# Key and query stacks of a transformer block: twelve SBUF-to-SBUF pieces, or three writes to DRAM and four reads back

## The chip, the cores and the metric

The kernel runs on one core of a Trainium2 chip. A core has TensorE (matrix multiplication; PE in the profile, its weight loads PEld), VectorE (DVE), ScalarE (ACT), GpSimd (POOL) and SyncE (SP), which here only issues transfers, and 16 DMA engines that carry them. The metric is the device time of one execution in microseconds. All times are of that chip; the profile is one execution recorded by the hardware.

## The reference

A pre-norm block with 2048 tokens, width 1024, 32 heads of 32, hidden width 3584, in float32. Its first part is attention over four segments of 512 tokens, with a memory matrix M carried from segment to segment:

```python
q, k, v = (x @ wq), (x @ wk), (x @ wv)        # per head, per segment of 512 tokens
for s in range(4):
    p = softmax(qs @ ks.T * Dh**-0.5 + causal_mask)
    a_dot = p @ vs
    a_mem = (phi(qs) @ M) / (phi(qs) @ z + 1e-6)
    o = g * a_mem + (1 - g) * a_dot
    M, z = M + phi(ks).T @ vs, z + phi(ks).sum(0)
h = x + concat(o) @ wo                         # x is layernormed before the projections
out = h + gelu(layernorm(h) @ w1 + b1) @ w2 + b2
```

The change concerns only `qs @ ks.T`, and only how its two operands get into place.

## The kernel before

**Precision.** Products that need more than the multiplier's reduced float32 format (fp32r) are made from halves: a value is split into `hi` (rounded to fp32r) and `lo` (the rest), and a product is hi·hi + hi·lo + lo·hi. In the projections these are three matmuls (`mm3`, L114–117). For the logits of one head the contraction has only 32 rows, so the three products are laid into one contraction of 96 rows: the key stack of a head holds its 32 rows of kh, kl, kh one under the other, the query stack those of qh, qh, ql. One matmul of 96 rows, L541, then gives all three products summed.

**Tiles.** The projections come out as `kps`, `qps`, `vps`: 128 rows (four heads of 32) by 512 tokens. ACT writes kh (L413) and qh (L427) out of PSUM, DVE makes kl (L414) and ql (L428). A head's rows lie at partitions 32j to 32j+31 there, and must be brought to partitions 0–31, 32–63 and 64–95 of that head's stack. Compute engines do not do that here; `stack` (L372) does it by transfers: for each of four heads a tile of 96 x 512 (`ks` or `qs`, five buffers each), filled by three DMAs of 32 x 512 (64 KB, L377), so twelve DMAs a stack, all issued by SP.

**Loops.** The attention runs in two halves of 1024 tokens, `attention(half)`. Within a half it goes over eight groups of four heads, and for each group over two segments `sl` = 0, 1. A pair of group and segment is a unit: 16 units in a half, 32 in all, with one key stack and one query stack each, 64 stacks. Units with `sl` 0 are called even here, those with `sl` 1 odd.

**What runs beside what.** `dense(g, sl, ws, u)` makes the projections of a unit in 24 steps, k, q and v in eight chunks of three matmuls. `heads(prev)` computes the attention of the unit before, head after head, in six small steps each (PLAN, L31). The two are interleaved one to one: while TensorE projects unit u it also does the logits, transposes and products of unit u − 1. `dense` calls for the key stack at the first chunk of the query projection and for the query stack at the first chunk of the value projection. Both are read first when the next unit begins, by the `qk` of head 0. In each half the first unit has no previous heads; it runs beside the layer norm of the other segment, and its stacks are needed soon after.

**Order.** A framework planned the instruction order of each engine when the kernel was built; on the chip each engine goes through its own list in that order and waits on semaphores. The SP list carries, beside the stacks: the weight blocks `wr<-wk/wq/wv` (L326, 512 KB each, two buffers, one trio per group, so in the odd units, each waiting until POOL or DVE has split the block whose buffer it takes, L92), the store of a unit's result `o_dram<-ot` (L609, 256 KB), rows of x for the residual (`ht`, L696), and at the end of a half the reads `orr<-o_dram` (L683) and the output weights `wr<-wo` (L700). Later parts of the kernel, the output projection and the two-layer perceptron, use the same queue but no stacks; they fill the time after about 500 us to 890 us and after 1400 us.

Of the kernel before, what the change touches and what calls it, by code (L numbers as in the profile page):

```python
# [10 lines left out]
F32 = mybir.dt.float32  # L11
# [28 lines left out]
def raw(ap):  # L40
    return ap.bitcast(F32)


def build(tc, x, wq, wk, wv, wo, beta, w1, b1, w2, b2, out):
    nc = tc.nc
    top = ExitStack()
    const = top.enter_context(tc.tile_pool(name="const", bufs=1))
    dram = top.enter_context(tc.tile_pool(name="dram", bufs=1, space=DRAM))
# [33 lines left out]
    p1_dram = [dram.tile([P, 512], F32, name=f"p1_dram{j}") for j in range(FB // 2)]  # L82
    h_dram = [[dram.tile([S // P, P, FB // 4, P], F32, name=f"h_dram{i}{s}") for s in range(2)] for i in range(2)]

    acts = {}

    def split(pool, w, hi, lo, hi_eng="vector", lo_eng="gpsimd"):
# [99 lines left out]
    def hooked(gen, fn, every, count):  # L187
        for n, _ in enumerate(gen):
            if n % every == every - 1 and n // every < count:
                fn(n // every)  # L190
            yield
# [152 lines left out]
    def attention(half, first):  # L344
# [26 lines left out]

        def stack(a, b, name, order):  # L372
            out = []
            for j in range(4):
                st = ab.tile([96, 512], F32R, tag=name, name=name, bufs=5)
                for blk, src in enumerate(order):
                    nc.sync.dma_start(raw(st[32 * blk:32 * blk + 32, :]), raw((a, b)[src][32 * j:32 * j + 32, :]))  # L377
                out.append(st)
            return out

# [21 lines left out]
        def dense(g, sl, ws, u):  # L402
# [15 lines left out]
            for c in project(ws["q"], sl, "qps", qps):  # L418
                if c == 0:
                    u["ks"] = stack(kh, kl, "ks", (0, 1, 0))  # L420
                if c == 2 and s < 3:
                    zc = ab.tile([P, 64], F32, name="zc", bufs=2)[:, 0:1]
                    pk = phi_sum(kparts, "pk", zc)
                next(behind, None)
                yield
# [7 lines left out]
            for c in project(ws["v"], sl, "vps", vps):  # L433
                if c == 0:
                    u["qs"] = stack(qh, ql, "qs", (0, 0, 1))
                if s > 0:
                    if c == 2:
                        pq = phi_sum(qparts, "pq")
                    if c == 4:
                        while small:  # L440
                            one_small()
                        pqh, pql = tmpr("pqh"), tmpr("pql")
                        mzh = ab.tile([P, 256], F32R, name="mzh", bufs=1)[:, 0:132]
                        mzl = ab.tile([P, 256], F32R, name="mzl", bufs=1)[:, 0:132]
                        nc.scalar.copy(pqh, pq)
                        nc.gpsimd.tensor_copy(mzh, MZ[:, g, :])
                        nc.gpsimd.tensor_tensor(mzl, MZ[:, g, :], raw(mzh), op=ALU.subtract)
                    if c == 5:
                        nc.gpsimd.tensor_tensor(pql, pq, raw(pqh), op=ALU.subtract)
                if c == 1 and s < 3:  # L450
                    pkn = ps_dense("pkn")
                    for i in range(4):
                        nc.tensor.transpose(pkn[:, i * P:(i + 1) * P], pk[:, i * P:(i + 1) * P], ident)
                    pkh, pkl = tmpr("pkh"), tmpr("pkl")
                    nc.scalar.copy(pkh, pkn)
                if c == 2 and s < 3:
                    nc.vector.tensor_tensor(pkl, pkn, raw(pkh), op=ALU.subtract)
                next(behind, None)
                yield
# [188 lines left out]
        for g in range(NG):  # L648
            for sl in range(2):
                u = {"g": g, "s": 2 * half + sl}  # L650
                d = dense(g, sl, ws, u)
# [6 lines left out]
                else:  # L658
                    if g == NG - 1 and sl == 1:
                        d = hooked(d, lambda k: load_o(half, 0, k, ab), 3, NG - 1)  # L660
# [19 lines left out]
    def load_o(half, sl, g, tp):  # L680
        oh, ol = o_tiles(half, sl)
        orr = tp.tile([P, 512], F32, tag="tmp", name="orr", bufs=5)
        nc.sync.dma_start(orr, o_dram[2 * half + sl][g])  # L683
        hi, lo = oh[:, g, :], ol[:, g, :]
        if sl == 0 and g % 2 == 0:
            nc.vector.tensor_copy(hi, orr)
        else:
            op = nc.scalar.copy(hi, orr)
            if sl == 1:
                tc.add_manual_dep(op.ins, acts["mm"].ins.name, NOSYNC, reason="program order")  # L690
        (nc.vector if g % 2 else nc.gpsimd).tensor_tensor(lo, orr, raw(hi), op=ALU.subtract)
# [613 lines left out]
    for half in range(2):  # L1305
# [53 lines left out]
        order = ExitStack()  # L1359
# [84 lines left out]
```

## Time and profile before

| | us |
|---|---|
| median of 3 runs | 2301.49 (2299.61 to 2301.78) |
| the profiled execution's span | 2296.2 |
| outside the span, against the median | 5.3 |
| TensorE busy | 2270.4 (99%) |
| VectorE busy | 1540.3 (67%) |
| ScalarE busy | 1225.0 (53%) |
| GpSimd busy | 1092.4 (48%) |

The span runs from the first to the last instruction that the profile records; busy times are sums over an engine's instructions in it. The profile's clock column for TensorE is full throughout. Rows of the timeline read: start in us from the span's start, duration in us, engine, line, operation, output<-input, and in square brackets how long the engine sat idle before and what ended that. "SPq" rows are DMA issues: their duration is what the issue took on SP, not what the transfer took. Rows of the list of DMA issues read: output<-input, issuing queue, operation, number, size of one, median us from issue to landing.

### The profile page before, as it was taken

How to read it: one execution, taken by the hardware profiler on the slowest of the kernel's cores; microseconds unless marked ns; L12 is line 12 of the kernel's file. 1: busy time of each engine (PE TensorE's matmuls, PEld its weight loads, DVE VectorE, ACT ScalarE, POOL GpSimd, SP SyncE). 2: the span in 40 equal slices, each digit the busy share in tenths (PEclk: the TensorE clock that was granted, in tenths of full speed). 3: DMA queues.
4: the chain of work that ended last, by engine and by line, in shares of the span. 5: the costliest groups of instructions: out<-in, count | busy, mean ns of one | idle time of the engine just before them, and what ended most of it. 6: DMA issues, size and time to landing. Idle time of an engine off the chain costs nothing.

```text
span 2296.2 us, 35279 instructions
## 1 busy us (share of the span) xinstructions
PE 2270.4 (99%) x11769; PEld 1890.8 (82%) x11769; DVE 1540.3 (67%) x3173; ACT 1225.0 (53%) x2549; POOL 1092.4 (48%) x1134
## 2 busy tenths in 40 slices
PE   8999999999999999999999999999999999999999
PEld 6888888878888888888888887888888888888887
DVE  6777777776655565777777777565566766577563
ACT  6777777775453445777777776363344223322221
POOL 5545555555244442555555556253445554155430
PEclk9999999999999999999999999999999999999999
DMA  6333333345465654433333344466667976476762
GB/s 190 92 85 91 93 89 85 87 120 182 139 204 172 188 165 142 113 91 86 85 87 88 87 111 140 156 211 175 176 188 263 345 243 216 159 253 221 249 234 90
DMA packets 322719, 355.36 MB, mean 155 GB/s; under 512 B 26190, under 2 KB 218730, under 8 KB 322538
## 3 DMA queue, kind: packets, MB, share of 16 engines
q1 hardware_dynamic: 259370, 316.40, 45.4%
q10 hardware_dynamic: 63168, 36.71, 5.3%
q8 instruction: 93, 1.52, 0.3%
q14 instruction: 88, 0.72, 0.1%
HBM read 226.59 MB, written 76.09 MB: 132 GB/s over the span
## 4 chain that ended last, share of the span: by engine, by line
PE 91%; ACT 3%; POOL 2%; DVE 2%; issue 1%; DMA 1%; ACTq 0%; SPq 0%; POOLq 0%; DVEq 0%
PE po L1278 22%; PE bps L882 9%; PE cps L882 7%; PE dps L882 6%; PE po L593 6%; PE ppt L573 6%; PE pqk L541 3%; PE vps L116 2%; PE vps L115 2%; PE kps L115 2%; PE kps L116 2%; PE vps L117 2%; PE kps L117 2%; PE pwo L117 2%; PE pwo L116 2%; PE pwo L115 2%
## 5 line engine op out<-in xcount | busy, mean ns | idle before, releaser
L557 POOL TENSOR_SCALAR pr<-pr,nm,gate 128x128 f32<-128x128 f32 (+3 forms) x512 | 322.6, 639 | 345.9 <-DVE nm L554 260.0
L550 ACT ACTIVATE pr<-pr,mx 128x256 f32<-128x256 f32 (+3 forms) x512 | 287.6, 562 | 161.9 <-DVE mx L542 158.2
L580 DVE TENSOR_TENSOR ptl<-ppt,pth 128x512 fp32r<-128x512 f32 (+1 forms) x384 | 227.2, 599 | 86.2 <-ACT pth L575 82.0
L542 DVE CUSTOM_DVE_ANT_0 pr<-pqk,mask 128x256 f32<-128x256 f32 (+3 forms) x512 | 243.3, 484 | 46.5 <-PE pqk L541 43.7
L573 PE MATMUL ppt<-ident,pr 128*128 128x128 f32 x1280 | 223.6, 277 | 2.1 <-POOL pr L557 1.4
L575 ACT CAST pth<-ppt 128x512 fp32r<-128x512 f32 (+1 forms) x384 | 194.2, 517 | 39.0 <-PE ppt L573 33.1
L1288 DVE TENSOR_TENSOR c<-c,po 128x512 f32<-128x512 f32 x160 | 105.4, 683 | 143.1 <-PE po L1278 135.5
L573 PEld LDWEIGHTS ppt<-ident,pr 128*128 128x128 f32 x1280 | 164.6, 140 | 32.5 <-POOL pr L557 2.6
L541 PE MATMUL pqk<-ks,qs 96*128 96x256 f32 (+3 forms) x512 | 161.3, 315 | 0.0
L92 POOL TENSOR_TENSOR wl<-wr,wh 128x1024 fp32r<-128x1024 f32 x52 | 124.5, 2393 | 70.8 <-PE pqk L541 27.6
L593 PE MATMUL po<-pth,vs 128*64 128x512 f32 (+3 forms) x512 | 155.4, 326 | 0.3 <-ACT pth L575 0.2
L593 PE MATMUL po<-ptl,vs 128*64 128x512 f32 (+3 forms) x512 | 153.9, 310 | 1.3 <-DVE ptl L580 1.2
L1278 PE MATMUL po<-w2h,zh 128*128 128x512 f32 x378 | 121.1, 390 | 0.8 <-DVE zh L1218 0.4
L1135 POOL TENSOR_TENSOR w2r<-w2r 128x512 f32<-128x512 f32 x54 | 85.4, 1593 | 72.0 <-DVE c L1288 36.9
L541 PEld LDWEIGHTS pqk<-ks,qs 96*128 96x128 f32 x512 | 96.2, 188 | 21.5
L994 POOL TENSOR_TENSOR s<-r 128x512 f32<-128x512 f32 x28 | 43.6, 1559 | 143.4 <-DVE sa L1010 87.1
L882 PE MATMUL bps<-zh,sb 128*128 128x512 f32 x336 | 111.0, 391 | 0.0
L882 PE MATMUL bps<-zh,sa 128*128 128x512 f32 x336 | 110.8, 390 | 0.0
L115 PE MATMUL vps<-yh,wh 128*128 128x512 f32 x256 | 109.4, 427 | 0.9 <-DVE MZ L497 0.9
L115 PE MATMUL kps<-yh,wh 128*128 128x512 f32 (+1 forms) x264 | 110.1, 417 | 0.0
L115 PE MATMUL qps<-yh,wh 128*128 128x512 f32 x256 | 106.8, 417 | 0.0
L1278 PE MATMUL po<-w2h,hl 128*128 128x512 f32 x322 | 103.2, 390 | 0.5 <-POOL hl L1218 0.3
(241 smaller groups left out, 6657.1 us busy)
## 6 DMA issues: line engine op xcount, KB each, us to landing
hr<-h_dram SPq DMA_DIRECT2D x112, 448.0 KB, 5.4
w2r<-in_B_w SPq DMA_DIRECT2D x122, 256.0 KB, 4.4
r<-in_B_w SPq DMA_DIRECT2D x56, 512.0 KB, 4.5
h_dram<-ht ACTq DMA_DIRECT2D x84, 256.0 KB, 3.7
ks<-kh SPq DMA_DIRECT2D x256, 64.0 KB, 2.0
qs<-qh SPq DMA_DIRECT2D x256, 64.0 KB, 2.0
wr<-in_A_wo SPq DMA_DIRECT2D x32, 512.0 KB, 4.0
wx<-in_B_w SPq DMA_DIRECT2D x56, 256.0 KB, 3.5
```

Source lines behind the costliest of these rows:

```text
L115: nc.tensor.matmul(ps, ah, bh, start=first, stop=False)
L116: nc.tensor.matmul(ps, ah, bl, start=False, stop=False)
L541: nc.tensor.matmul(pqk[:, :n], u["qs"][j][:, i * P:(i + 1) * P], u["ks"][j][:, 0:n], start=True, stop=True)
L542: nc.vector.tensor_tensor_reduce(out=st["pr"][:, offs[i]:offs[i] + n], in0=pqk[:, :n], in1=mask[:, 512 - n:512], op0=ALU.add, op1=ALU.min, ...
L550: nc.scalar.activation(pi, pi, AF.Exp, bias=mx[:, i:i + 1], scale=-1.0, accum_out=mx[:, 4 + i:5 + i])
L557: nc.gpsimd.tensor_scalar(pi, pi, nm[:, 4 + k:5 + k], gate[:, 1, 4 * g + j:4 * g + j + 1], op0=ALU.mult, op1=ALU.mult)
L573: nc.tensor.transpose(ppt[:, o:o + P], pr[:, offs[i] + jk * P:offs[i] + (jk + 1) * P], ident)
L575: acts["pth"] = n, nc.scalar.copy(pth[:, base:base + w], ppt[:, :w])
L580: nc.vector.tensor_tensor(o, x0, x1, op=ALU.subtract)
L593: nc.tensor.matmul(po[:, P * jk:], v, st[part][:, koff[jk]:koff[jk] + w], start=(jk, part) == (0, "pth"), stop=(jk, part) == (2, "ptl"))
L882: nc.tensor.matmul(ps, x_[:, c, :], y_[:, c, :], start=first and c == 0 and n == 0, stop=last and c == 3 and n == 2, skip_group_check=True)
L1278: nc.tensor.matmul(ps, x_[:, k], y_[k], start=opens and k == 0 and i == 0, stop=closes and k == self.KP - 1 and i == 2, skip_group_check=True)
```

## The change

Each stack goes through DRAM. Two DRAM tiles for the keys and two for the queries, used in turn, have the shape 4 heads x 3 blocks x 32 rows x 512. For each of the three blocks one DMA writes the half that belongs there, for all four heads at once: the source is the whole tile of 128 x 512 (256 KB), and in the destination each head's 32 rows lie together (64 KB), the four heads 192 KB apart. Then, for each head, one DMA reads its three blocks, 96 rows that lie together in DRAM (192 KB), into the stack tile. So a stack takes three writes and four reads, seven DMAs in place of twelve, all still on SP; every byte is moved twice. A read waits until the writes that it depends on have landed, and a write waits for the reads of the stack before the last one, which used the same DRAM tile.

```diff
+    s_dram = {n: [dram.tile([4, 3, 32, 512], F32, name=f"{n}_dram{k}") for k in range(2)] for n in ("ks", "qs")}
     acts = {}
...
         def stack(a, b, name, order):
             out = []
+            n = acts[name] = acts.get(name, 0) + 1
+            d = s_dram[name][n % 2]
+            for blk, src in enumerate(order):
+                nc.sync.dma_start(d[:, blk], raw((a, b)[src]))
             for j in range(4):
                 st = ab.tile([96, 512], F32R, tag=name, name=name, bufs=5)
-                for blk, src in enumerate(order):
-                    nc.sync.dma_start(raw(st[32 * blk:32 * blk + 32, :]), raw((a, b)[src][32 * j:32 * j + 32, :]))
+                nc.sync.dma_start(raw(st), d[j].rearrange("b r n -> (b r) n"))
                 out.append(st)
             return out
```

In the built program the matrix, vector, scalar and GpSimd instructions keep their order, but for TensorE at the first units of the two halves and around the output projection, where the plan places some other matmuls ahead. On SP an even unit's list is: three key writes, three key reads, the store of `ot`, the fourth key read, three query writes, four query reads. An odd unit's is: three key writes, `wr<-wv`, three key reads, the store, the fourth key read, three query writes, `wr<-wk`, four query reads, `wr<-wq`. In the changed kernel's profile the lines behind L377 stand four lower: the stack's writes are L378, its reads L381, the logits' matmul L545. Lines between L82 and L377 move by one.

## The prediction

> **What bounds the kernel now.** I read the page first (busy time, then the chain that ended last), then the list of DMA issues, then the timeline around three boundaries between units. All rows are of the one profiled execution, span 2296.2 us.
>
> ```profile
> PE 2270.4 (99%) x11769; PEld 1890.8 (82%) x11769; DVE 1540.3 (67%) x3173; ACT 1225.0 (53%) x2549; POOL 1092.4 (48%) x1134
> PE 91%; ACT 3%; POOL 2%; DVE 2%; issue 1%; DMA 1%; ACTq 0%; SPq 0%; POOLq 0%; DVEq 0%
> L541 PE MATMUL pqk<-ks,qs 96*128 96x256 f32 (+3 forms) x512 | 161.3, 315 | 0.0
> ```
>
> TensorE is the bound: 2296.2 − 2270.4 = 25.8 us idle in all, and DMA is 1% of the chain. The matmul that reads the two stacks, L541, never sat behind anything (last column 0.0). So the stacks cost nothing today; a gain can come only out of those 25.8 us, and a loss has no such limit, because TensorE works in a written order and stops at the first L541 whose stack has not landed.
>
> The change sits in the transfers of L377. Columns: KB of one, median us from issue to landing.
>
> ```profile
> ks<-kh SPq DMA_DIRECT2D x256, 64.0 KB, 2.0
> qs<-qh SPq DMA_DIRECT2D x256, 64.0 KB, 2.0
> wr<-in_A_wk SPq DMA_DIRECT2D x16, 512.0 KB, 4.4
> h_dram<-hb SPq DMA_DIRECT2D x16, 512.0 KB, 3.1
> o_dram<-ot SPq DMA_DIRECT2D x28, 256.0 KB, 2.3
> orr<-o_dram SPq DMA_DIRECT2D x28, 256.0 KB, 3.2
> b1r<-in_B_b SPq DMA_DIRECT2D x1, 14.0 KB
> ```
>
> **How much room each stack has.** The key stack is asked for at the first step of the query projection and the query stack at the first step of the value projection; both are first read at the next unit's first L541. The query stack is the tight one. First an even unit (segment 0 of a group) of the first half: ACT makes qh, DVE ql, SP issues pieces, TensorE reads.
>
> ```profile
> 274.59 0.59 ACT L427 CAST qh<-qps 128x512 fp32r<-128x512 f32 x1
> 275.13 0.58 SPq L377 DMA_DIRECT2D ks<-kh  x1
> 275.21 0.69 DVE L428 TENSOR_TENSOR ql<-qps,qh 128x512 fp32r<-128x512 f32 x1
> 275.81 1.17 SPq L377 DMA_DIRECT2D qs<-qh  x2
> 277.09 0.52 SPq L377 DMA_DIRECT2D qs<-ql  x1
> 283.95 0.28 PE L541 MATMUL pqk<-ks,qs 96*128 96x256 f32 x1
> ```
>
> From qh (274.59 + 0.59 = 275.18) to the first L541 at 283.95 are 8.8 us. Head 0 needs three pieces; the last is issued at 277.09 and lands 2.0 us later, near 279.1: 4.9 us to spare. The other heads follow about 7.5 us apart, so head 0 decides.
>
> An odd unit (segment 1) of the first half, and both kinds in the second half:
>
> ```profile
> 293.29 0.56 ACT L413 CAST kh<-kps 128x512 fp32r<-128x512 f32 x1
> 303.42 0.39 PE L541 MATMUL pqk<-ks,qs 96*128 96x512 f32 x1
> 304.44 0.58 ACT L427 CAST qh<-qps 128x512 fp32r<-128x512 f32 x1
> 304.67 2.40 POOL L92 TENSOR_TENSOR wl<-wr,wh 128x1024 fp32r<-128x1024 f32 x1 [1.12 <-PE pqk L541]
> 313.86 0.28 PE L541 MATMUL pqk<-ks,qs 96*128 96x256 f32 x1
> ```
>
> ```profile
> 962.41 0.58 ACT L427 CAST qh<-qps 128x512 fp32r<-128x512 f32 x1
> 971.77 0.28 PE L541 MATMUL pqk<-ks,qs 96*128 96x256 f32 x1
> 980.73 0.59 ACT L413 CAST kh<-kps 128x512 fp32r<-128x512 f32 x1 [1.14 <-PE kps L117]
> 993.70 0.59 ACT L427 CAST qh<-qps 128x512 fp32r<-128x512 f32 x1
> 1002.70 0.28 PE L541 MATMUL pqk<-ks,qs 96*128 96x256 f32 x1
> ```
>
> The room is 8.8 us in both even units, 313.86 − 305.02 = 8.8 us and 1002.70 − 994.29 = 8.4 us in the odd ones.
>
> **The change, part by part.**
>
> Issues. A stack falls from twelve issues to seven; at 0.58 us (the row at 275.13) that takes 2.9 us of SP's time off each of 64 stacks. SP is not on the chain, so I count nothing for it; what it could bring is the second rival.
>
> Order. After the three writes SP stands until they have landed, because the first read waits for all three. Behind it wait, in odd units, the output store o_dram, the fourth key read and the query writes. The wk load goes out between query writes and reads and waits for POOL's wl (304.67 + 2.40 = 307.07), which ends before the writes can land: nothing. ACT, DVE and POOL keep their order; TensorE's differs at the two starts and beside the output projections.
>
> One write. It moves 256 KB out of 128 rows into a destination whose outermost count is four: one 64 KB block per head, 192 KB apart, and inside it 32 rows. How many of the 16 engines share it is the question. These two windows hold one store and one read of DRAM; the last two columns are the DMA share and GB/s.
>
> ```profile
> 268.90:269.40 0.50, 0.50 (x5) 0.41 (x4) 0.33 (x2) 0.47 (x3) 0.06 (x1) 1.00 0.68 254
> 470.60:472.20 1.60, 1.60 (x11) 1.18 (x10) 0.60 (x5) 0.99 (x4) 0.00 (x0) 1.00 0.88 288
> ```
>
> One engine moves 254 / (16 x 0.68) = 23.3 GB/s in the first and 288 / (16 x 0.88) = 20.5 in the second. So 256 KB on all 16 engines take 0.7 us, and o_dram's 2.3 us are 1.6 us fixed and 0.7 us of data. On four engines they take 64 KB / 23.3 = 2.8 us (3.2 at 20.5).
>
> The bounds for the three writes of a stack, from the first issue: on 16 engines 2 x 0.6 + 2.3 = 3.5 us; on four, which they would share one behind the other, 1.6 + 3 x 2.8 = 10.0 us (11.2 at the slower rate). I take four. Nearest in the list is b1r, 28 rows and not 128 or 32: it alone has no landing time, so a transfer's outermost count does show in how it is carried out, and every row with 128 outermost behaves as one spread evenly.
>
> [...]
>
> One read: 96 rows, 192 KB. Between 2.0 us (a 64 KB piece) and 3.0 us (orr's 3.2 less a quarter of its 0.8 of data at 20.5 GB/s); I take 2.6.
>
> Sum of a steady boundary. From query half to stack: 10.0 + 2.6 = 12.6 us.
> - Even units: 12.6 − 8.8 = 3.8 us of stall.
> - Odd, second half: the key stack's writes begin at kh, 981.32, land at 991.3; five issues (three reads, o_dram, the fourth read) of 0.6 us free SP at 994.3, just as qh comes: 12.6 − 8.4 = 4.2 us.
> - Odd, first half: kh at 293.85, landed 303.85, SP free at 306.9, 1.9 us after qh (305.02): 12.6 + 1.9 − 8.8 = 5.7 us. The fourth read's own wait (for the L541 at 303.42) is over by then.
>
> The stall comes once per boundary and moves all that follows by as much. Sixteen units in each half make 14 even and 14 odd steady boundaries beside the starts and ends: 14 x 3.8 + 7 x 4.2 + 7 x 5.7 = 122 us.
>
> The starts, where nothing covers the stacks.
>
> ```profile
> 25.19 0.56 ACT L413 CAST kh<-kps 128x512 fp32r<-128x512 f32 x1
> 38.97 0.28 PE L541 MATMUL pqk<-ks,qs 96*128 96x256 f32 x1
> 900.08 0.56 ACT L413 CAST kh<-kps 128x512 fp32r<-128x512 f32 x1
> 912.95 0.34 PE L541 MATMUL pqk<-ks,qs 96*128 96x256 f32 x2
> ```
>
> First half: kh 25.75, key writes landed 35.8, four reads issued by 38.2, query writes landed 48.2, stack 50.8. TensorE has 14 more matmuls ahead of that L541 than before, at the page's 2270.4 / 11769 = 0.19 us some 2.7 us, so it arrives at 41.7: 9 us lost. Second half: 900.64, 910.6, 913.0, 923.0, 925.6 against some 914.7 (I allow 1.8 us of moved matmuls): 11 us. Two x loads stand between query writes and reads and add up to 1.4 us at each. Together 20.
>
> The two ends: stalls of 3 to 5 us, but there TensorE already idles.
>
> ```profile
> 480.00:525.00 45.00, 41.01 (x241) 32.54 (x240) 34.31 (x97) 33.50 (x81) 27.77 (x35) 1.00 0.55 166
> 1350.00:1395.00 45.00, 41.41 (x246) 33.21 (x245) 34.76 (x100) 33.50 (x80) 27.57 (x32) 1.00 0.49 147
> ```
>
> That idle time (45.00 − 41.01 = 4.0 us, and 3.6 us) takes up part: 0 to 4 us each, I take 2.
>
> Sum: 122 + 20 + 4 = 146 us on the span of 2296.2. The median of the runs, 2301.49, lies 5.3 us above the span, for what is around it; I add the sum to the median: **2447 us**.
>
> **The rivals.**
>
> *All engines share a write; no change.* The store rows (o_dram 256 KB in 2.3 us, hb 512 KB in 3.1) speak for it, but all have 128 rows outermost. The stack is there 3.5 + 2.6 = 6.1 us after qh, with 8.8 and 8.4 of room; odd units of the first half add nothing (key writes landed by 297.4). The starts lose about 1 us each: 2303 us.
>
> *Faster.* The place is the two windows at the output projection. With 16 engines SP gets 5 issues, 2.9 us a stack, earlier to the reads of o_dram and the wo loads behind the last stacks; if those loads are what TensorE idles for, up to 4.0 + 3.6 = 7.6 us go: 2294 us. It decides from 4.6 us on. Against it: TensorE's longest waits in these windows (total, times, longest) are short and for DVE, not for a transfer.
>
> ```profile
> PE po L593 <- DVE ptl L580: 0.9, 2, 0.5
> PE pm L395 <- DVE rg L483: 1.1, 1, 1.1
> ```
>
> [...]
>
> *Half-way: the three writes overlap on different engines, or four engines move more than 23.3 GB/s each because twelve are silent.* If one 256 KB write took 2.0 us, the chain would be 1.6 + 6.0 + 2.6 = 10.2 us: 1.4 to 1.8 us a boundary, 45 us in all, starts 15: 2361 us. No row speaks for or against.
>
> **How the numbers follow.** Four engines 0.78 (own range 2395 to 2505: 0.9 us less per chain to 1.2 to 2.4 us more, over 28 boundaries), half-way 0.08 (2310 to 2395), no change 0.10, faster 0.04. A change under 0.2%, 4.6 us, is about what a measurement here cannot tell from none. The first two cases are slower: 0.86; same 0.10; faster 0.04. To leave out no more than 2 in 10, the range takes in the four-engine case and the upper part of the half-way one: 2345 to 2505 us.
>
> **What would show it.** In the profile after, the query stack's reads (L381) are DMA issues of 192 KB at 2 to 3 us; the writes (L378), 256 KB, show 4 us or more, or no landing time as b1r; a window that holds only writes shows a DMA share near 0.25. L545, as L541 is then called, has idle time before it of some 140 us, released by the DMA of qs, and TensorE's busy time stays near 2270 in a longer span. A boundary follows the last after some 35 us, where 971.77 and 1002.70 are 31 apart. If the writes land in about 2.3 us, the step "four engines" is wrong and the time is that of the first rival. If they are slow and the time still does not move, my room of 8.8 us is wrong. If the wait stands at the key reads, or at the output projection, I have put the stall in the wrong place.

## The result, and the profile after

The changed kernel takes 2745.3 us (2740.19 to 2746.58), the kernel before 2300.55 us in the same comparison: a ratio of 1.193, 95% interval 1.191 to 1.195. It is slower, by 445 us, three times the 146 us of the forecast and far above the range's upper end of 2505 us. The profiled execution spans 2742.7 us.

From the page of the changed kernel: busy times, the TensorE clock in 40 slices, the chain that ended last, and the group of the logits' matmul (now L545; the last part is its idle time before and what ended most of it).

```profile
PE 2413.5 (88%) x11769; PEld 1969.7 (72%) x11769; DVE 1541.8 (56%) x3173; ACT 1227.1 (45%) x2549; POOL 1089.8 (40%) x1134
PEclk8888989888899999898898988889999999999999
PE 67%; DMA 23%; ACT 3%; DVE 2%; SPq 2%; issue 2%; POOL 1%; ACTq 0%; POOLq 0%; DVEq 0%
L545 PE MATMUL pqk<-ks,qs 96*128 96x256 f32 (+3 forms) x512 | 180.9, 355 | 174.2 <-DMA qs<-qs_dram 172.2
```

Two things have changed on TensorE, not one. Its idle time is 2742.7 − 2413.5 = 329 us in place of 25.8. And the same 11769 matmuls are busy for 2413.5 us in place of 2270.4: 143 us that no transfer explains directly. DMA, 1% of the chain before, is 23%.

What waits for what, in the changed kernel (us in total, times, longest):

```profile
PE pqk L545 <- DMA qs<-qs_dram: 172.2, 31, 17.5
PE po L597 <- DVE ot L608: 83.9, 26, 5.0
ACT ot L602 <- DMA o_dram<-ot: 151.0, 26, 7.8
SPq L381 <- DMA ks_dram<-kh: 194.4, 30, 9.4
```

The first row is the wait that was forecast. The next two are another one: ACT may not write the next result into `ot` before the store of the last has left it, and TensorE in the end waits for that. The tile `ot` has one buffer. The fourth row is why: SP stands for the landing of the key writes, and the store is behind it. One boundary from the timeline, in order of time:

```profile
372.83 1.05 SPq L378 DMA_DIRECT2D ks_dram<-kh  x1
382.83 1.25 SPq L381 DMA_DIRECT2D ks<-ks_dram  x3
384.17 0.38 SPq L613 DMA_DIRECT2D o_dram<-ot  x1
389.71 0.58 ACT L602 COPY ot<-po 32x512 f32<-32x512 f32 x1 [5.74 <-DMA o_dram<-ot]
390.31 0.59 ACT L431 CAST qh<-qps 128x512 fp32r<-128x512 f32 x1
390.92 1.08 SPq L378 DMA_DIRECT2D qs_dram<-qh  x2
391.05 0.69 PE L597 MATMUL po<-pth,vs 128*64 128x512 f32 x1 [3.08 <-DVE ot L608]
392.04 0.56 SPq L378 DMA_DIRECT2D qs_dram<-ql  x1
402.17 1.72 SPq L381 DMA_DIRECT2D qs<-qs_dram  x4
404.73 0.58 PE L545 MATMUL pqk<-ks,qs 96*128 96x256 f32 x1 [5.40 <-DMA qs<-qs_dram]
```

SP issues the last key write at 372.83, the first key read ten us later, and the store behind that. The first stall of TensorE is 3.08 us, the second 5.40. From the first query write to the first read are 402.17 − 390.92 = 11.25 us, from there to the matmul 2.6 us.

Windows of the changed kernel; the last three columns are the granted clock, the DMA share and GB/s:

```profile
396.00:398.00 2.00, 2.00 (x12) 1.66 (x11) 1.97 (x4) 1.81 (x5) 0.20 (x1) 1.00 0.26 102
402.20:403.00 0.80, 0.00 (x0) 0.00 (x0) 0.00 (x0) 0.00 (x0) 0.00 (x0) 0.50 0.00 0
405.00:407.00 2.00, 2.00 (x7) 1.51 (x8) 0.70 (x4) 0.60 (x2) 0.00 (x0) 0.50 0.42 139
407.00:409.00 2.00, 2.00 (x10) 1.53 (x9) 0.20 (x3) 0.49 (x2) 0.99 (x2) 0.72 0.00 0
409.00:411.00 2.00, 2.00 (x17) 1.86 (x15) 1.43 (x4) 1.53 (x3) 0.00 (x0) 1.00 0.00 0
1235.60:1765.30 529.70, 426.29 (x2256) 343.89 (x2256) 283.38 (x834) 273.24 (x690) 205.51 (x276) 0.88 0.32 96
```

The first row, while only query writes are in flight, has a DMA share of 0.26, which is that of four engines of sixteen (0.25), at 102 GB/s or 102 / (16 x 0.26) = 24.5 GB/s each. The next four are the clock: after some 3 us of idle TensorE (it stands from 399.33) the clock is 0.50 and stays there after the restart at 404.73. The mean of 0.72 from 407 to 409 puts its return at about 408.1 (1.1 us at 0.50 and 0.9 at 1.00), 3.4 us after the restart; from 409 it is full throughout. That costs about 0.5 x 2.3 + 0.28 x 2 = 1.7 us for this stall. The last row runs from the third unit of the second half to the fifteenth, twelve boundaries: 35.5 us busy and 8.6 us idle each, against 30.8 us and nothing in the same stretch before:

```profile
971.80:1341.30 369.50, 369.50 (x2257) 313.11 (x2256) 279.80 (x835) 272.66 (x692) 208.36 (x277) 1.00 0.34 86
```

In the list of DMA issues of the changed kernel no row has a landing time any more, those of other transfers included:

```profile
ks_dram<-kh SPq DMA_DIRECT2D x64, 256.0 KB
qs<-qs_dram SPq DMA_DIRECT2D x128, 192.0 KB
o_dram<-ot SPq DMA_DIRECT2D x28, 256.0 KB
```

The time of a write had therefore to be read off the distance between the issue of the first write and that of the first read, which waits for all three.

### The profile page after: what moved, and what is told of

Read it like the earlier page. It is cut to its first block, busy times and chain, and to the rows that moved or that the text cites. A ratio compares the mean times of both kernels' runs of the same rounds, so it can differ in the third digit from the quotient of the medians.

```text
span 2742.7 us, 34605 instructions
## 1 busy us (share of the span) xinstructions
PE 2413.5 (88%) x11769; PEld 1969.7 (72%) x11769; DVE 1541.8 (56%) x3173; ACT 1227.1 (45%) x2549; POOL 1089.8 (40%) x1134
## 4 chain that ended last, share of the span: by engine, by line
PE 67%; DMA 23%; ACT 3%; DVE 2%; SPq 2%; issue 2%; POOL 1%; ACTq 0%; POOLq 0%; DVEq 0%
PE po L1282 19%; DMA qs_dram<-ql 12%; PE bps L886 8%; PE cps L886 6%; PE dps L886 5%; PE po L597 4%; DMA o_dram<-ot 4%; PE ppt L577 3%; DMA qs<-qs_dram 3%; PE pqk L545 2%; PE kps L116 2%; PE kps L117 2%; PE kps L118 2%; PE pwo L117 2%; PE pwo L118 2%
## 5 line engine op out<-in xcount | busy, mean ns | idle before, releaser
L545 PE MATMUL pqk<-ks,qs 96*128 96x256 f32 (+3 forms) x512 | 180.9, 355 | 174.2 <-DMA qs<-qs_dram 172.2
L545 PEld LDWEIGHTS pqk<-ks,qs 96*128 96x128 f32 x512 | 109.2, 214 | 215.4 <-DMA qs<-qs_dram 85.2
L597 PE MATMUL po<-pth,vs 128*64 128x512 f32 (+3 forms) x512 | 180.0, 373 | 91.5 <-DVE ot L608 83.9
L577 PE MATMUL ppt<-ident,pr 128*128 128x128 f32 x1280 | 238.1, 290 | 24.7 <-DVE ptl L584 18.0
L597 PE MATMUL po<-ptl,vs 128*64 128x512 f32 (+3 forms) x512 | 177.9, 355 | 15.0 <-DVE ptl L584 13.1
L597 PEld LDWEIGHTS po<-pth,vs 128*64 128x64 f32 x512 | 79.6, 155 | 129.8 <-DVE ot L608 90.6
L608 DVE TENSOR_TENSOR ot<-po,ot 32x512 f32<-32x512 f32 x128 | 87.2, 681 | 145.1 <-ACT ot L602 142.1
L602 ACT COPY ot<-po 32x512 f32<-32x512 f32 x128 | 73.9, 578 | 154.6 <-DMA o_dram<-ot 151.0
L117 PE MATMUL kps<-yl,wh 128*128 128x512 f32 (+1 forms) x264 | 113.7, 431 | 0.7 <-DVE yl L278 0.6
L118 PE MATMUL kps<-yh,wl 128*128 128x512 f32 (+1 forms) x264 | 112.3, 425 | 0.0
```

The costliest lines, as they stand in the source:

```text
L117: nc.tensor.matmul(ps, ah, bl, start=False, stop=False)
L118: acts["mm"] = nc.tensor.matmul(ps, al, bh, start=False, stop=last)
L545: nc.tensor.matmul(pqk[:, :n], u["qs"][j][:, i * P:(i + 1) * P], u["ks"][j][:, 0:n], start=True, stop=True)
L577: nc.tensor.transpose(ppt[:, o:o + P], pr[:, offs[i] + jk * P:offs[i] + (jk + 1) * P], ident)
L597: nc.tensor.matmul(po[:, P * jk:], v, st[part][:, koff[jk]:koff[jk] + w], start=(jk, part) == (0, "pth"), stop=(jk, part) == (2, "ptl"))
```

## The experiments

The table gives the median time; the mean distance between the first logits' matmuls of successive units, from the third unit to the fifteenth of each half; and the median distance from a query stack's first write to its first read, in even and odd units, where there is one (from half to half, where those differ). The last two are worked out from the starts in each trace's timeline.

| kernel | us | boundary, 1st half | 2nd half | first write to first read |
|---|---|---|---|---|
| before | 2300.6 | 30.95 | 30.79 | |
| changed | 2745.3 | 44.74 | 44.14 | 11.4 / 12.1 |
| e8: eight blocks outermost | 2468.0 | 35.01 | 35.32 | 7.2 / 8.4 |
| e16: 128 rows outermost | 2325.7 | 30.95 | 30.80 | 3.5 to 4.4 / 3.7 to 3.8 |
| eks: key stacks alone | 2498.0 | 36.74 | 37.14 | |
| eqs: query stacks alone | 2583.6 | 39.39 | 39.58 | 11.4 / 12.1 |
| estore: store issued by ScalarE | 2675.0 | 41.79 | 41.04 | 11.8 to 11.9 / 12.2 to 13.2 |
| eksst: eks, store by ScalarE | 2358.4 | 31.6 | 31.5 | |
| eqsfill: eqs, stall filled with matmuls | 2546.0 | 37.79 | 38.12 | 11.4 / 12.2 |
| hyb: e16, but pieces at starts and ends | 2302.0 | 30.94 | 30.80 | |

**How many engines carry a write: e16 and e8.** In e16 the DRAM tile is laid out with head and row outermost and the three blocks inside; sizes, transfers and their order stay.

```diff
-dram.tile([4, 3, 32, 512], F32, name=f"{n}_dram{k}")
+dram.tile([4 * 32, 3, 512], F32, name=f"{n}_dram{k}")
...
-nc.sync.dma_start(raw(st), d[j].rearrange("b r n -> (b r) n"))
+nc.sync.dma_start(raw(st), d[32 * j:32 * j + 32].rearrange("r b n -> (r b) n"))
```

> The changed kernel with another layout of the DRAM tiles, 128 rows outermost (head and row together), the three blocks inside: a write has 128 rows, 1536 elements apart, as its outermost count, a read is still 96 rows that lie together (the 96 rows of a contraction come in another order, the same for keys and queries). Same transfers, same bytes, same order on every engine. Theory 'four engines': a write is spread over 16, three of them land 3.5 to 3.7 us after the first issue, stack 6.2 us after qh with 8.4 to 8.8 us of room: no stall at the boundaries, the store of a unit's result leaves before the next unit wants its buffer, TensorE's clock stays at 1.00: 2301 us, within 2296 to 2306. Rival 'the way through DRAM itself' (a write, its landing and a read in a row on SP cost this much whatever the engines): near 2745 us.

Measured: 2325.67 us, 1.011 times before (1.009 to 1.012); TensorE's order is that of the changed kernel to the last instruction. The landing times are back:

```profile
PE 2280.0 (98%) x11769; PEld 1897.5 (82%) x11769; DVE 1541.9 (66%) x3173; ACT 1225.8 (53%) x2549; POOL 1090.6 (47%) x1134
qs_dram<-qh SPq DMA_DIRECT2D x64, 256.0 KB, 2.4
qs<-qs_dram SPq DMA_DIRECT2D x128, 192.0 KB, 3.6
```

A write takes 2.4 us, and the boundaries are as far apart as before, 30.95 and 30.80 us: nothing is lost or won there. 420 of the 445 us hang on the layout of the destination alone; the way through DRAM as such is ruled out for them. The other 24 us I had expected at 2. They lie outside the steady part: the second unit's first logits' matmul is 8.3 us late, the third of the second half 23.5, and from there on it stays at that to the fifteenth.

e8 puts eight blocks of 16 rows outermost:

```diff
+dram.tile([8, 3, 16, 512], F32, name=f"{n}_dram{k}")
...
+nc.sync.dma_start(raw(st), d[2 * j:2 * j + 2].rearrange("h b r n -> (h b r) n"))
```

> The same with 8 blocks of 16 rows outermost (each head's stack as two times three blocks of 16 rows). Theory 'four engines', in its general form (the outermost count sets the number): eight engines carry a write, DMA share 0.50 while they do; at 20.5 GB/s of one engine 32 KB take 1.6 us, three writes 1.6 + 4.8 = 6.4 us, stack 9.0 us after qh against 8.4 to 8.8 of room: stalls of 0.2 to 0.6 us a boundary, a little more at the starts: 2315 us (2300 to 2335). Rival 'the way through DRAM itself': near 2745 us.

Measured: 2467.99 us, 1.072 (1.070 to 1.075). A window of e8 while only query writes are in flight, and its largest wait:

```profile
392.00:393.00 1.00, 1.00 (x10) 0.92 (x10) 0.73 (x3) 0.12 (x2) 0.56 (x2) 1.00 0.51 195
PE pqk L545 <- DMA qs<-qs_dram: 71.0, 30, 10.0
```

The share is 0.51, which is that of eight engines of sixteen (0.50), as expected for eight blocks outermost. So outermost counts of 4, 8 and 128 give a share of 0.26, one of 0.51 and no stall, and the three writes take 11.4, 7.2 and about 3.7 us. The time missed my 2315: three writes took 7.2 to 8.4 us and not 6.4, with the clock's price on top. The boundaries cost 28 x 4.3 = 120 of the 166 us; the rest is at the starts and ends.

**Which stack costs what: eks and eqs.** One of the two goes through DRAM, the other by pieces as before. The diff is that of eks; eqs has "qs" in both places.

```diff
+            if name == "ks":
+                n = acts[name] = acts.get(name, 0) + 1
+                d = s_dram[name][n % 2]
+                for blk, src in enumerate(order):
+                    nc.sync.dma_start(d[:, blk], raw((a, b)[src]))
             for j in range(4):
                 st = ab.tile([96, 512], F32R, tag=name, name=name, bufs=5)
+                if name == "ks":
+                    nc.sync.dma_start(raw(st), d[j].rearrange("b r n -> (b r) n"))
+                else:
+                    for blk, src in enumerate(order):
+                        nc.sync.dma_start(raw(st[32 * blk:32 * blk + 32, :]), raw((a, b)[src][32 * j:32 * j + 32, :]))
```

> Only the key stacks go through DRAM (four blocks outermost), the query stacks are copied in twelve pieces as before. Theory of two waits: SP stands some 10 us for the landing of the key writes, the store of the unit's result behind it comes late and ACT's write of the next result waits for it (3.1 us of idle TensorE a boundary in the changed kernel, and some 2 us more at the lower clock after it); the query pieces are in time: 28 x 5 = 140 us, and at the starts some 10: 2450 us. If that second wait only follows from the late query stack: 2301 to 2315 us.

> Only the query stacks go through DRAM, the key stacks are copied in pieces as before. Theory of two waits: the wait at the first logits' matmul stays, 5.4 to 5.9 us a boundary plus some 2.5 us at the lower clock after it, the wait for the store goes: 28 x 8.1 = 227 us and 10 at the starts: 2540 us. With the run on the keys alone the two losses add up to the whole 445 us, to 60. If the query stack alone is the cause: near 2745 us.

Measured: eks 2498.03 us (1.086, 1.084 to 1.087), eqs 2583.61 us (1.123, 1.121 to 1.124). The losses, 196 and 282 us, add up to 478, near the 445 of both; each is some 45 us above what I expected of it. The waits of eks:

```profile
PE po L602 <- DVE ot L613: 80.9, 26, 5.0
ACT ot L607 <- DMA o_dram<-ot: 148.1, 26, 7.7
```

and of eqs:

```profile
PE pqk L550 <- DMA qs<-qs_dram: 145.0, 24, 7.8
```

The two waits come apart cleanly: the one for the store belongs to the key stacks, though TensorE never waits for a key stack in the steady part; the one for the query stack to the query stacks.

**The store behind SP's wait: estore and eksst.** One word changes in each, `nc.sync` to `nc.scalar` at the store of `ot`.

> The changed kernel, with one edit: the store of a unit's result (o_dram from ot, 256 KB) is issued by ScalarE and no longer stands on SP behind the landing of the key writes. Theory 'second wait': ACT's wait for that store (151 us in the changed kernel) and TensorE's wait for ot behind it (84 us) go to under 20 us, and with them the lower clock after them; the run on the keys alone priced this at 196 us less some 10 at its starts, so 2745 - 186 = 2560 us (2530 to 2610). Rival: the store lands late because its engines are busy with the writes, whoever issues it: above 2700 us.

> The kernel with only the key stacks through DRAM on four engines (2498.0 us), with the store of a unit's result issued by ScalarE. TensorE's order is the same as in that run. Theory 'SP stands for the landing, the store behind it is late, ACT waits for the store's buffer': the wait for ot (81 us on TensorE, 148 on ACT) goes, the clock stays at 1.00, the query pieces come 1 to 2 us later than before and have 4.9 us to spare: only the starts are left, 2320 us (2305 to 2345). If the store is late because its engines carry the key writes, not because of SP: above 2440 us.

estore: 2675.0 us, a gain of 70 us and not 186. eksst: 2358.41 us, a gain of 140 us over eks. Waits of estore, then a window of eksst:

```profile
PE pqk L545 <- DMA qs<-qs_dram: 234.8, 30, 16.8
SPq L381 <- DMA ks_dram<-kh: 207.8, 30, 11.4
```

```profile
1100.00:1400.00 300.00, 295.08 (x1780) 246.24 (x1778) 224.25 (x664) 216.40 (x547) 162.04 (x220) 1.00 0.39 109
```

In eksst TensorE's wait for `ot` is gone, the clock is full and a boundary costs 0.7 us more than before in place of 6.1: the store was late because of its place on SP, behind the wait for the key writes. At the boundary shown above it left late, at 384.17, and then took 5.5 us behind three reads until ACT could go on; the runs do not price the two apart. The rest of eksst's 58 us is at the starts and ends of the halves, more than the 20 I gave it. In estore the wait for `ot` is gone too, but two thirds of the gain are given back one wait later: SP waits up to 11.4 us for the key writes in place of 9.4 (the store is now in flight with them, presumably the reason), the query writes follow up to 1.8 us after qh in place of at once, and TensorE's wait for the query stack grows from 172 to 235 us. It seems that the stall that came first had hidden part of the second.

**The lower clock: eqsfill.** To eqs, 22 matmuls are added in front of the matmul that waits.

```diff
+if i == 1 and j == 0 and not (u["g"] == NG - 1 and u["s"] % 2):
+    yf = acts["y", u["s"] % 2][0]
+    for k in range(22):
+        nc.tensor.matmul(pqk, yf[:, k % DC, 0:P], yf[:, k % DC, 0:512], start=True, stop=True)
 nc.tensor.matmul(pqk[:, :n], u["qs"][j][:, i * P:(i + 1) * P], u["ks"][j][:, 0:n], start=True, stop=True)
```

> The kernel with only the query stacks through DRAM (2583.6 us), and in front of the first logits' matmul of each unit but a half's last, 22 matmuls whose result is overwritten by it (operands that are there already; 30 x 22 x 0.23 us = 150 us more work for TensorE). They fill the time in which TensorE waits for the query stack (5.5 to 7.8 us). Theory 'idle lowers the clock': TensorE is granted half its clock after an idle stretch and takes some us to get back; filled, the clock stays near 1.00 and a boundary gets some 2.5 us shorter: 2509 us (2490 to 2535), though the kernel does more. Rival 'the busy time grew for another reason' (operands come later, work spreads out): no gain, 2584 us or more.

Measured: 2546.02 us, 38 us faster than eqs with 150 us more of work. A stretch of the second half, first of eqs, then of eqsfill:

```profile
1200.00:1500.00 300.00, 247.41 (x1404) 205.57 (x1403) 175.84 (x523) 171.94 (x435) 131.99 (x172) 0.91 0.32 90
```

```profile
1200.00:1500.00 300.00, 287.35 (x1645) 240.09 (x1645) 186.68 (x548) 179.16 (x454) 136.87 (x182) 0.98 0.32 89
PE pqk L554 <- DMA qs<-qs_dram: 40.7, 25, 6.9
```

The clock rises from 0.91 to 0.98, and a boundary shrinks by 1.5 us though its query stack comes no sooner (11.4 and 12.1 or 12.2 us in both). Between the third unit and the fifteenth, the matmuls that run at half clock cost 2.2 us a boundary in eqs and 0.3 in eqsfill, added up from the clock records of the two traces. So the longer busy time does come from the idle time before it. The gain is half of the 75 us expected: the matmuls fill about 5 us of stalls of 5.5 to 7.8, and TensorE still waits 40.7 us for query stacks, where it waited 145.0.

How the clock moved in the changed kernel: it was 0.50 after a stall whose idle time was 3.08 us (0.53 in the microsecond after 391.0), and full again about 3.4 us after the restart at 404.73.

**Is the way through DRAM worth anything: hyb.** e16, but the first and last unit of each half build their stacks from pieces.

```diff
+u = acts["units"] = acts.get("units", 0) + 1
+if (u - 1) % 32 < 2 or (u - 1) % 32 >= 30:
+    for j in range(4):
+        st = ab.tile([96, 512], F32R, tag=name, name=name, bufs=5)
+        for blk, src in enumerate(order):
+            nc.sync.dma_start(raw(st[32 * blk:32 * blk + 32, :]), raw((a, b)[src][32 * j:32 * j + 32, :]))
+        out.append(st)
+    return out
```

> The layout with 128 rows outermost (the run at 2325.7 us), but the first and the last unit of each half build their stacks out of twelve pieces as in the kernel before. In that run all of the 24 us are lost at the two starts (8 us each) and behind the two last units (5 us each), nothing at the 28 boundaries between. Theory: in the steady part the way through DRAM with 16 engines is hidden and brings nothing: 2301 us (2296 to 2306), no change. If the five issues a stack fewer on SP are worth something: below 2296 us.

Measured: 2302.01 us against 2302.12, ratio 0.9999 (0.9990 to 1.0008): no change. e16's 24 us lay wholly in those four units. Whether late stacks cost them, or the other order of TensorE's instructions there, is open: hyb restores both. In the other 28 a stack by seven transfers and one by twelve cost the same, nothing; the issues saved on SP bring nothing. No version tried is faster than the kernel before.

## Why the prediction was wrong

The direction was right, and so was the mechanism of the wait that was forecast: TensorE stands 174 us in front of L545, where some 140 were forecast. But that is two fifths of the loss. The span grew by 446.5 us: 143 of busy time, 174 of idle time in front of L545, 84 in front of L597 for `ot`, and 45 of other idle time (329 − 25.8 − 174 − 84). The clock and the store were no terms of the sum. Step by step:

- *What bounds the kernel.* Right: TensorE, 99% busy, so there was little to gain and hyb gained nothing.
- *A write gets four engines.* Right, but it was an estimate: no row of before shows a transfer on four engines, or three writes that share them. The runs show it: the share of 0.26, which stays between 0.24 and 0.26 from 392 to 401.5 us with all three writes issued by 392.6, and the 0.51 of e8. In e16 three writes take about 3.7 us.
- *Three writes 10.0 us, read 2.6.* The read was 2.6 to 2.8 (no row of before shows one of 96 rows; the DMA share is 0.87 from 403 to 404 us, with only the four query reads in flight). The writes took 11.4 to 12.1, the upper bound (11.2) and beyond. From qh to the matmul are mostly 14.0 to 15.0 us, against 8.4 to 8.8 of room. The idle time in front of the 28 boundaries' L545 is 140 us, 5.0 each; 4.4 each, 122 us, were forecast. This term was mis-sized, but only by 18 us.
- *Odd units of the first half 1.9 us later.* Wrong: query writes there follow qh at once. SP was indeed held, but qh itself came late, for the reason of the next point. In estore, where that reason is gone, they follow qh by 0.8 to 1.2 us in most odd units of the first half.
- *Order: "Behind it wait, in odd units, the output store o_dram, the fourth key read and the query writes."* This is one of the two steps that failed. I listed the store (it stands there in even units too) and counted the time that SP needs for it, but did not follow who waits for it: ACT, to write `ot` again, and TensorE behind ACT. Price: 83.9 / 26 = 3.2 us a time of idle TensorE, with the slow clock behind it; eks, which has this wait alone, loses 196 us.
- *"TensorE's busy time stays near 2270."* The other step that failed, and the larger missing term. I took a stall to cost its own length. TensorE's busy time grew by 143 us in all, 35.5 − 30.8 = 4.7 us a boundary. Added up from the clock records of the trace, matmuls ran for 262 us at half clock, which makes 131 of the 143.
- *Starts and ends, 24 us.* 28 boundaries x (44.44 − 30.87) make 380 us; the other 65 lie at the starts and ends. The idle time in front of L545 at the two starts is 32 us, where 20 were forecast. The sum there had the same missing terms, but I did not take the rest apart.
- *Idle time of some 140 us in front of L545.* It is 174 us, and another 155 us of idle time lie elsewhere.
- *"ACT, DVE and POOL keep their order".* So they do between the starts and ends, and TensorE too. At the starts and around the output projections the traces show all four with some instructions in another order; no run prices that by itself.
- *Own range 2395 to 2505.* Its lower end does not follow from its terms: 28 x 0.9 = 25 us less is 2422.

A boundary costs 13.6 us more, between the third unit and the fifteenth, on average of both halves: 5.1 of idle time in front of L545 for the query stack, 3.5 in front of the products of L597, nearly all for `ot`, 0.3 of other idle time, and 4.7 of longer busy time, 4.2 of it at half clock. Of the rivals, "all engines share a write" is what e16 is, and its 2303 us was low by the 24 us at starts and ends; "half-way" needed three writes in 7.6 us, and they took 11.4; nothing in any run speaks for "faster".

## What to carry to other kernels

Look at the outermost count of the transfer that fills a DRAM tile: here the same bytes took 2745 us with 4, 2468 with 8 and 2326 with 128, the only counts measured, and a DMA share of 0.26 with nothing else in flight gave the fault away. When an issuing queue is made to stand for a landing, follow everything behind it to the buffer that it frees and to the engine that writes that buffer next (140 us between eks and eksst). And price a stall of TensorE at its length plus the slow clock afterwards, where the trace shows one: here about 2 us a stall (4.2 us for the two stalls of a boundary in the changed kernel, 3.08 and 5.40 us long at the one shown, and 2.2 for the one of eqs, 5.5 to 7.8 us long).

## What the runs showed of the hardware that was not expected

- In the changed kernel, eks and eqs (four blocks outermost) and in e8 (eight) no transfer in the list of DMA issues has a landing time; in e16 every one but b1r has it again, as in the kernel before (2.4 us for a write of qh). Why is open.
- A store of 256 KB issued at 384.17 behind three reads of 192 KB on the same queue freed its buffer only at 389.7: 5.5 us, against a median of 2.3 us to landing in the kernel before.
- The clock had fallen some 2 us into a stall: in the changed kernel TensorE stands from 399.33, and the clock is 1.00 until 401.3 and 0.50 from 401.4. In the stall before, 3.08 us from 387.97, it was still 1.00 until 391.0.
- More work made a kernel faster: 660 added matmuls, 38 us less.
